# FNet mixing followed by an ELU layer in float32: the second layer's products as pairs of 64-column array tiles

## The chip, the cores and the metric

The kernel runs on one core of a Trainium2 chip. The metric is the device time of one execution in microseconds (us); lower is better. A span in a profile runs from the first to the last instruction of one profiled execution.

## What is computed

Everything is float32. For 8 sequences of 3008 rows with 256 channels, the reference takes the real part of a two-dimensional Fourier transform and feeds the resulting 24064 rows of 256 numbers to a two-layer network with 2048 hidden columns and an ELU between the layers:

```python
X = np.fft.fft(x, axis=1)
X = np.fft.fft(X, axis=2).real        # (8, 3008, 256) -> rows of 256
h = rows @ w_in                       # w_in 256 x 2048
g = np.where(h > 0.0, h, np.exp(np.minimum(h, 0.0)) - 1.0)
out = g @ w_out                       # w_out 2048 x 256
```

## The kernel before

**Symmetry.** The real transform is symmetric: row k and row 3008 - k come from the same two parts, a sum and a difference. So the kernel works on 8 x 1504 = 12032 columns, each standing for a pair of rows, and produces both rows of the pair. The channel transform is folded into the first layer's weights (`Wc`, `Ws`), and the sequence transform is done by matmuls with constant cosine and sine matrices (`MC`), whose results lie in two ring buffers `Rr` and `Ir`.

**Steps.** The columns are cut into 47 tiles of 256 (`TW`). For each tile there are 8 steps, 376 in all; a step handles two blocks of 128 hidden columns. In a step, TensorE does this:

- `mm_P` (L646): two products `H<-Rr,Wc`, each 128 weight columns by 256 moving columns, into a PSUM bank `H`.
- `mm_X1` (L739): three products of the second layer, for the step two periods earlier, into the banks pA and pB.
- `mm_Q` (L649): two products `H<-Ir,Ws`, added to the same bank `H`.
- `mm_X2` (L747): the other four products of the second layer, into pC and pD.

So a step has 4 products of the first layer and 7 of the second. The 7 stand for 8 block products: two hidden blocks times two output halves for each of the pair's two rows, combined in Strassen's way. The combined activations are seven blocks of 256 columns in the tile `G` (`blk(S, j)`, made by VectorE's ELU at L672 and by GpSimd's sums at L703 to L718, which all pass through the helper line L311), and the combined weights are `WT` (L358) beside the plain `w2`. A product of the second layer adds to one half, 256 columns, of a PSUM bank of 512 columns. The four banks pA to pD gather eight steps; then VectorE and ScalarE combine and transpose them (L757 to L800), and SyncE stores the rows.

All second-layer products go through one function, `prod` (L719). Its arguments are the accumulator bank `a`, the bank's half, the weights `lhsT` (128 x 128) and the number `j` of the block of G. All matmuls go through the helper `mm` (L300), so the profile shows them under L302 and they must be told apart by their tiles.

In float32 each matmul of the program runs as two weight loads (PEld LDWEIGHTS) and two matmul instructions (PE MATMUL): the profile's `x1504` for `H<-Rr,Wc` is 376 steps x 2 products x 2.

**Order.** The order on every engine is the program's order, written out by hand: each piece of a step has a due time (a list at L945 to L963, period 4.8), the pieces are sorted by it, and every instruction is pinned in that order. On TensorE the steady order is P, X1, Q, X2, P, and so on, with the sequence transform of a later sequence (`H<-MC,...`, some 28 of the steps carry a piece) between an X2 and the next P.

**Column tiles that are there already.** Four pieces use fewer than 128 weight columns and put their results in different 32-partition strips of one bank, so that they address different column tiles of the array: `dft_ext` (L561, 8 weight columns), `mid_mm` (L846), `mid_out` (L863) and `mid_pick` (L879), with 32 weight columns each. Each runs once. A fifth kind, `set_rest` (L461) and `whole_bank` (L895), multiplies one row of zeros.

Of the kernel before, what the change touches and what calls it, by code (L numbers as in the profile page):

```python
# [23 lines left out]
TW = 256  # L24
# [62 lines left out]
def kernel(  # L87
# [76 lines left out]
    w1 = {}  # L164

    class Chunk:
        """512 columns of weights: given as float64 words, they are rounded to the nearest
        float32 on chip; given as float32, they are loaded as they are."""

        def __init__(self, src, dst, raw, tmp):  # L170
            self.src, self.dst, self.raw_tags, self.tmp_tag = src, dst, raw, tmp
# [12 lines left out]
            )  # L184

        def parts(self):
            """low and high words, and the target, in columns of one shape"""
            dst = self.dst()
            raw = self.raw.rearrange("p (a b) w -> p a b w", a=dst.shape[1])
            return raw[:, :, :, 0], raw[:, :, :, 1], dst  # L190

        def fields(self):
            """The power of two 2^e as float32 bits (0 below float32's range); the low word
            as a fraction; the top 20 bits of the mantissa at float32's place."""
            if not wide:
                return
            lo, hi, dst = self.parts()
            t = spool.tile([128, 512], I32, tag=self.tmp_tag, bufs=1, name="pow2")
            self.t = t.rearrange("p (a b) -> p a b", a=dst.shape[1])
            pin(  # L200
                nc.vector.tensor_scalar(  # L201
                    out=self.t, in0=hi, scalar1=20, scalar2=0x7FF,
                    op0=ALU.logical_shift_right, op1=ALU.bitwise_and,
                )
            )
            act(self.t, self.t, func=AF.Relu, scale=2.0**23, bias=ebias)
            act(lo.bitcast(FP), lo.bitcast(U32), scale=2.0**-52)
            pin(
                nc.vector.tensor_scalar(
                    out=dst.bitcast(I32), in0=hi, scalar1=3, scalar2=0x7FFFF8,  # L210
                    op0=ALU.logical_shift_left, op1=ALU.bitwise_and,
                )
            )

        def join(self):
            """2^e * (1 + top bits) is exact; adding 2^e * the rest rounds."""
            if not wide:
                return
            lo, hi, dst = self.parts()
            vtt(dst.bitcast(I32), dst.bitcast(I32), self.t, ALU.bitwise_or)  # L220
            gtt(lo.bitcast(FP), lo.bitcast(FP), self.t.bitcast(FP), ALU.mult)
            gtt(lo.bitcast(FP), lo.bitcast(FP), dst, ALU.add)
# [77 lines left out]
    def mm(out_, lhsT, rhs, start, stop=True):  # L300
        pin(
            nc.tensor.matmul(  # L302
                out_, lhsT=lhsT, rhs=rhs, start=start, stop=stop, skip_group_check=True
            )
        )

    def vtt(o, a, b, op):
        pin(nc.vector.tensor_tensor(out=o, in0=a, in1=b, op=op))  # L308

    def gtt(o, a, b, op):  # L310
        pin(nc.gpsimd.tensor_tensor(out=o, in0=a, in1=b, op=op))  # L311

    def act(o, i, func=AF.Copy, **kw):
        pin(nc.scalar.activation(out=o, in_=i, func=func, **kw))  # L314


    def fold_weights():
        """w_in behind the channel DFT's cosine and sine halves."""
        n = len(w1_chunks)
        for c in range(n + 2):  # L320
            if c < n:
                if c >= 4:
                    w1_chunks[c].load()
                w1_chunks[c].fields()
            if 1 <= c <= n:
                w1_chunks[c - 1].join()
            if c >= 2:
                w1_chunks[c - 2].sign()
            if c >= 3 and c % 2:
                fold_block((c - 3) // 2)  # L330
        spread_last_row()

    def fold_block(q):
        cols = slice(q * 512, (q + 1) * 512)
        for part, dst in ((128, Ws), (0, Wc)):
            ps = bank("H")
            for h in range(2):
                mm(
                    ps,
                    CC[:, h * 256 + part : h * 256 + part + 128],  # L340
                    w1[q][:, h],
                    h == 0,
                    h == 1,
                )
            act(dst[:, cols], ps)

    def spread_last_row():
        nc.gpsimd.dma_start(out=wx_dr, in_=Ws[127:128, :])
        with nc.allow_non_contiguous_dma(reason="one row to columns"):
            nc.gpsimd.dma_start(  # L350
                out=wex, in_=wx_dr.rearrange("o (f p) -> p (o f)", p=128)
            )
# [307 lines left out]
        vtt(two(S.G[:, 0:512])[:, :, ::-1], two(S.E), two(S.H), ALU.subtract)  # L660

    def below(o, h):
        """max(-h, 0), so that exp(-o) = exp(min(h, 0)) cannot overflow."""
        act(o, h, func=AF.Relu, scale=-1.0)

    def exp_neg(ap):
        act(ap, ap, func=AF.Exp, scale=-1.0)

    def elu(o, h, e):
        """max(exp(min(h, 0)) - 1, h): exp(h) - 1 >= h, and 0 < h for positive h."""  # L670
        pin(
            nc.vector.scalar_tensor_tensor(  # L672
                out=o, in0=e, scalar=-1.0, in1=h, op0=ALU.add, op1=ALU.max
            )
        )

    def below_plus(i):
        S = steps[i]
        below(S.G[:, 512:1024], S.H)

    def below_minus(i):
        S = steps[i]
        S.M = bank("M")
        below(S.M, S.G[:, 0:512])
# [7 lines left out]
    def g_plus(i):  # L692
        S = steps[i]
        elu(S.G[:, 512:1024], S.H, S.G[:, 512:1024])

    def g_minus(i):
        S = steps[i]
        elu(S.G[:, 0:512], S.G[:, 0:512], S.M)

    def blk(S, j, n=1):  # L700
        return S.G[:, j * TW : (j + n) * TW]
# [16 lines left out]

    def prod(i, a, half, lhsT, j):  # L719
        S, T = steps[i], tiles[i // 8]  # L720
        mm(
            T.acc[a][:, half * TW : (half + 1) * TW],
            lhsT,
            blk(S, j),
            i % 8 == 0 and half == 0,
            i % 8 == 7,
        )

    def w2b(i, r, c):
        f = 2 * (i % 8) + r  # L730
# [8 lines left out]
    def mm_X1(i):  # L739
        if i % 8 == 0:  # L740
            T = tiles[i // 8] = Tile()
            T.acc = [bank(t) for t in ACC[0:2]]
        prod(i, 0, 0, w2b(i, 0, 0), 0)
        prod(i, 1, 0, w2b(i, 1, 0), 1)
        prod(i, 1, 1, wt(i, 1), 2)
# [107 lines left out]
    def mid_below():  # L853
        t = spool.tile([128, HALF + 1], FP, tag="rx", bufs=1, name="mid")
        state["mh"], state["mr"] = t[:, 0:512], t[:, 512:1024]
        below(state["mr"], state["mid"])

    def mid_g():
        h, r = state["mh"], state["mr"]
        elu(h, state["mid"], r)  # L860
        pin(nc.vector.transpose(out=r, in_=h))
# [38 lines left out]
    for _ in range(8):  # L900
        mm(bank("M"), zero[:, 0:128], zero[:, 0:1].to_broadcast([1, 512]), True)
    exp_neg(warm)
    fold_weights()
    EO, ops = fold_x(L_first, nc.vector, 1)

# [35 lines left out]
    T = PERIOD  # L941
# [192 lines left out]
```

## Time and profile before

| | |
|---|---|
| median of 2 runs | 2079.44 us (2078.43 and 2080.45) |
| span of the profiled execution | 2078.8 us |
| PE busy (matmuls, ends modelled) | 1983.5 us, 95% of the span, 8842 instructions |
| PEld busy (weight loads) | 1663.2 us, 80%, 8842 instructions |
| ScalarE, GpSimd, VectorE busy | 1393.9, 1385.7 and 976.6 us |
| mean granted TensorE clock | 0.983 |
| starts of step to step, steps 40 to 375, most of them | 4.753 us |

The span of the profiled execution is 0.6 us below the median of the runs; no other time is recorded for that execution, so sums below are made against 2078.8 us. PE means matmuls and PEld weight loads; these overlap. [...]the durations of successive matmuls overlap too: the distance between their starts tells their cost, and the duration doesn't. In a line such as `H<-w,mid 128*32 128x256 f32 x32`, 128*32 means 128 rows and 32 columns of weights, 128x256 the moving operand, and x32 the number of instructions.

### The profile page before, as it was taken

The page shows a single profiled execution, that of the slowest core. Times are in us where ns is not written, and L with a number is a line of the kernel's source. Part 1 is how long each engine was busy: PE and PEld are TensorE (multiplying, and loading weights), DVE is VectorE, ACT ScalarE, POOL GpSimd, SP SyncE. Part 2 cuts the span into 40 slices and gives each one's busy share as a digit, 9 for nine tenths or more (in the row PEclk, how much of TensorE's full clock was granted, in tenths as well). Part 3 has the DMA queues.
Part 4 walks back from the last instruction along what each step waited for, and adds up shares of the span by engine and source line. Part 5 has one row for each costly group of instructions (what it writes and reads, how often), then busy time and mean ns, then how long its engine had stood idle before and what let it go on. Part 6 is the DMA issues. An engine that isn't in the chain of part 4 may idle for free.

```text
span 2078.8 us, 27261 instructions
## 1 busy us (share of the span) xinstructions
PE 1983.5 (95%) x8842; PEld 1663.2 (80%) x8842; DVE 976.6 (47%) x1589; ACT 1393.9 (67%) x2761; POOL 1385.7 (67%) x1874
## 2 busy tenths in 40 slices
PE   3568999999999999999999999999999999999997
PEld 1247888888888888888888888888888888888886
DVE  2654454445444544454445445444544454445444
ACT  2255676777667766677667776677766776667775
POOL 3378775778657775678657786577756776555664
PEclk8799999999999999999999999999999999999999
DMA  8710211112100111012001120011110010100101
GB/s 217 117 51 11 57 49 16 16 33 62 23 11 18 46 44 23 11 22 77 11 19 20 35 57 18 15 17 54 42 24 11 18 18 17 16 11 11 21 11 21
DMA packets 253848, 71.07 MB, mean 34 GB/s; under 512 B 242370, under 2 KB 243162, under 8 KB 253194
## 3 DMA queue, kind: packets, MB, share of 16 engines
q1 hardware_dynamic: 251290, 56.73, 14.2%
q0 software_dynamic: 2416, 12.61, 1.9%
q8 instruction: 70, 1.15, 0.2%
q14 instruction: 72, 0.59, 0.1%
HBM read 44.45 MB, written 24.80 MB: 33 GB/s over the span
## 4 chain that ended last, share of the span: by engine, by line
PE 90%; DMA 2%; POOL 2%; DVE 2%; SPq 1%; ACT 1%; issue 1%; DVEq 0%; POOLq 0%; ACTq 0%
PE H L302 37%; PE pB L302 15%; PE pC L302 15%; PE pD L302 15%; PE pA L302 8%; DMA raw<-in_moe_w_out_dram 1%; POOL raw L311 1%; SPq L526 1%; DMA raw<-in_moe_w_in_dram 1%; POOL G L311 1%; DVE e L380 0%; DVE pow L201 0%; DVE w L229 0%; ACT G L314 0%; POOL WT L311 0%
## 5 line engine op out<-in xcount | busy, mean ns | idle before, releaser
L311 POOL TENSOR_TENSOR G<-G 128x256 f32<-128x256 f32 x1504 | 1080.5, 729 | 608.0 <-DVE G L672 473.6
L672 DVE SCALAR_TENSOR_TENSOR G<-G,H 128x512 f32<-128x512 f32 x376 | 258.5, 688 | 917.8 <-ACT G L314 917.7
L314 ACT ACTIVATE E<-H 128x512 f32<-128x512 f32 x376 | 224.5, 597 | 333.7 <-PE H L302 333.7
L302 PE MATMUL H<-Rr,Wc 128*128 128x256 f32 x1504 | 394.2, 385 | 8.8 <-ACT H L314 8.6
L302 PE MATMUL H<-Ir,Ws 127*128 127x256 f32 x1504 | 390.6, 382 | 1.4 <-ACT E L314 1.4
L302 PE MATMUL pC<-G,WT 128*128 128x256 f32 x1504 | 389.1, 381 | 0.0
L314 ACT ACTIVATE G<-H 128x512 f32<-128x512 f32 x376 | 224.6, 597 | 236.5 <-DVE G L308 236.5
L314 ACT ACTIVATE H<-Rb,wex 128x256 f32<-128x256 f32 x752 | 354.9, 472 | 16.9 <-DMA Rb<-r 3.1
L302 PEld LDWEIGHTS H<-Rr,Wc 128*128 128x128 f32 x1504 | 280.5, 190 | 54.1 <-ACT H L314 11.4
L302 PEld LDWEIGHTS H<-Ir,Ws 127*128 127x128 f32 x1504 | 287.6, 191 | 43.2 <-ACT E L314 2.5
L302 PEld LDWEIGHTS pC<-G,WT 128*128 128x128 f32 x1504 | 287.2, 191 | 40.7
L672 DVE SCALAR_TENSOR_TENSOR G<-M,G 128x512 f32<-128x512 f32 x376 | 256.9, 683 | 0.0
L308 DVE TENSOR_TENSOR G<-E,H 128x512 f32<-128x512 f32 x376 | 254.6, 677 | 4.6 <-PE H L302 4.0
L302 PE MATMUL pB<-G,WT 128*128 128x256 f32 x752 | 225.8, 382 | 16.7 <-POOL G L311 16.6
L314 ACT ACTIVATE G<-G 128x512 f32<-128x512 f32 x376 | 234.5, 624 | 0.0
L302 PE MATMUL pA<-G,w 128*128 128x256 f32 x752 | 224.4, 380 | 4.5 <-DVE G L672 2.4
L302 PE MATMUL pD<-G,WT 128*128 128x256 f32 x752 | 224.6, 380 | 0.0
L302 PE MATMUL pB<-G,w 128*128 128x256 f32 x752 | 224.1, 380 | 0.0
L302 PE MATMUL pD<-G,w 128*128 128x256 f32 x752 | 224.0, 380 | 0.0
L314 ACT ACTIVATE M<-G 128x512 f32<-128x512 f32 x376 | 224.0, 596 | 0.0
L314 ACT ACTIVATE M<-M 128x512 f32<-128x512 f32 x376 | 222.2, 591 | 0.0
L302 PEld LDWEIGHTS pB<-G,WT 128*128 128x128 f32 x752 | 142.8, 191 | 38.8 <-POOL G L311 19.7
(116 smaller groups left out, 1523.6 us busy)
## 6 DMA issues: line engine op xcount, KB each, us to landing
out_dram<-ot SPq DMA_DIRECT2D x504, 32.0 KB
xl<-in_x_dram SPq DMA_DIRECT2D x16, 768.0 KB
MC<-dft_mats SPq DMA_DIRECT2D x4, 1131.0 KB
raw<-in_moe_w_in_dram SPq DMA_DIRECT2D x8, 512.0 KB
raw<-in_moe_w_out_dram SPq DMA_DIRECT2D x8, 512.0 KB
out_dram<-ot SPq DMA_DIRECT2D x256, 2.0 KB
Rb<-r SPq DMA_DIRECT2D x10, 376.0 KB
out_dram<-ot SPq DMA_DIRECT2D x64, 28.0 KB
```

The source lines that it names most:

```text
L302: nc.tensor.matmul(out_, lhsT=lhsT, rhs=rhs, start=start, stop=stop, skip_group_check=True)
L308: pin(nc.vector.tensor_tensor(out=o, in0=a, in1=b, op=op))
L311: pin(nc.gpsimd.tensor_tensor(out=o, in0=a, in1=b, op=op))
L314: pin(nc.scalar.activation(out=o, in_=i, func=func, **kw))
L526: nc.sync.dma_start(out=t[:, s0:s1], in_=bass.AP(tensor=xt, offset=x.offset + row * ND + 128, ap=[[SEQ * ND, NB], [step * ND, s1 - s0], [1 ...
L672: nc.vector.scalar_tensor_tensor(out=o, in0=e, scalar=-1.0, in1=h, op0=ALU.add, op1=ALU.max)
```

## The change

Each second-layer product, 128 weight columns by 256 moving columns, is cut into four matmuls of 64 weight columns by 128 moving columns. The inner loop over `r` puts the two halves of the weight columns into partitions 0 to 63 and 64 to 127 of the accumulator, so into two different column tiles of the array; the outer loop over `c` cuts the moving columns. The mark that starts an accumulation goes to the first moving half alone. The weights, the blocks of G, the accumulators, the due times and everything outside `prod` stay as they are. Some docstrings are taken out as well, which makes no instruction and is left out here.

```diff
     def prod(i, a, half, lhsT, j):
         S, T = steps[i], tiles[i // 8]
-        mm(
-            T.acc[a][:, half * TW : (half + 1) * TW],
-            lhsT,
-            blk(S, j),
-            i % 8 == 0 and half == 0,
-            i % 8 == 7,
-        )
+        for c in range(2):
+            for r in range(2):
+                o = half * TW + c * 128
+                mm(
+                    T.acc[a][64 * r : 64 * r + 64, o : o + 128],
+                    lhsT[:, 64 * r : 64 * r + 64],
+                    S.G[:, j * TW + c * 128 : j * TW + c * 128 + 128],
+                    i % 8 == 0 and half == 0 and c == 0,
+                    i % 8 == 7,
+                )
```

In the changed program the matmuls of TensorE stand in the same order, with four in the place of each one of the second layer. The wait that stood before a product (for VectorE, or for GpSimd) stands before the first of its four. The order on the other engines is unchanged.

## Prediction

> **What bounds the kernel now.** I read the share of busy time, then the windows, then the list of waits, then the timeline of one step. The windows say where TensorE is the bound (columns: window, us, busy us of PE with its count, PEld, DVE, ACT, POOL, granted clock, DMA share, GB/s):
>
> ```profile
> 200.00:600.00 400.00, 398.13 (x1785) 337.02 (x1784) 185.59 (x305) 278.63 (x555) 280.97 (x379) 1.00 0.15 33
> 600.00:1000.00 400.00, 400.00 (x1819) 343.41 (x1818) 189.19 (x308) 287.15 (x571) 288.44 (x393) 1.00 0.15 33
> 1000.00:1400.00 400.00, 400.00 (x1798) 338.26 (x1797) 189.31 (x313) 278.37 (x555) 270.68 (x371) 1.00 0.12 25
> ```
>
> PE never stops at full clock; ScalarE and GpSimd work 70% of the time and VectorE 47%. The list of waits gives the whole kernel only 16.6 us of PE waiting for GpSimd before a second-layer product, and that falls before 210 us. So from about 180 us to the end, time added on TensorE is added to the kernel, and the other engines' work has room. The timeline of matmuls shows a step (start us, us from first start to last end):
>
> ```profile
> 1201.19 1.03 PE L302 MATMUL H<-Rr,Wc 128*128 128x256 f32 x4
> 1202.05 0.59 PE L302 MATMUL pA<-G,w 128*128 128x256 f32 x2
> 1202.48 0.59 PE L302 MATMUL pB<-G,w 128*128 128x256 f32 x2
> 1202.92 0.59 PE L302 MATMUL pB<-G,WT 128*128 128x256 f32 x2
> 1203.35 1.03 PE L302 MATMUL H<-Ir,Ws 127*128 127x256 f32 x4
> 1204.21 1.03 PE L302 MATMUL pC<-G,WT 128*128 128x256 f32 x4
> 1205.08 0.59 PE L302 MATMUL pD<-G,WT 128*128 128x256 f32 x2
> 1205.51 0.59 PE L302 MATMUL pD<-G,w 128*128 128x256 f32 x2
> 1205.94 0.38 PE L302 MATMUL H<-Rr,Wc 128*128 128x256 f32 x1
> ```
>
> From 1201.19 to 1205.94 is 4.75 us for 22 matmul instructions: 216 ns from start to start (0.86 us for four, 0.43 for two).
>
> The second thing to read is what a column tile costs here. The kernel has one run of 32-column tiles, the timeline of matmuls around `mid_out`, and the weight loads of the same stretch:
>
> ```profile
> 1889.76 0.59 PE L302 MATMUL pD<-G,w 128*128 128x256 f32 x2
> 1890.28 1.93 PE L302 MATMUL H<-w,mid 128*32 128x256 f32 x32
> 1892.15 0.70 PE L302 MATMUL H<-Rr,Wc 128*128 128x256 f32 x2
> ```
> ```profile
> 1890.28 1.45 PEld L302 LDWEIGHTS H<-w,mid 128*32 128x32 f32 x32 [0.33 <-PE pD L302]
> 1892.15 0.51 PEld L302 LDWEIGHTS H<-Rr,Wc 128*128 128x128 f32 x3 [0.41 <-issue]
> ```
>
> 32 matmuls of 256 columns start within 1.93 - 0.38 = 1.55 us. One after another they would take 32 x 0.216 = 6.9 us: four tiles run together, 8 rounds of 0.216. But the crossings cost. The last full matmul starts at 1889.76 + 0.22 = 1889.97, the first tiled one 0.31 us later in place of 0.216; on the way back the last tiled one starts at 1891.84, and the full one again 0.31 us later. A narrower window shows four tiled matmuls started by 1890.30, with 0.40 us each in place of 0.38: 24 ns of exposed weight load. The two full ones after the crossing take 0.70 in place of 0.59 us: 104 ns exposed. The rows by form give the loads' durations:
>
> ```profile
> L302 PEld LDWEIGHTS H<-Rr,Wc 128*128 128x128 f32 x1504 | 280.5, 190 | 54.1 <-ACT H L314 11.4 <-issue 2.3 <-ACT M L314 0.4
> ...
> L302 PEld LDWEIGHTS H<-w,mid 128*32 128x32 f32 x32 | 0.9, 109 | 0.8 <-PE pD L302 0.3
> ```
>
> [...](190 - 109) / 96 = 0.84 ns per column, on top of some 82 ns that don't delay the next load.[...]
>
> **The change part by part.**
>
> 1. *Tiled products.* 376 x 7 = 2632 products have 2 matmul instructions each, 5264; they become 8 each, 21056. They run in pairs, so a product is 4 rounds of 128 columns.[...] 4 x 109.4 = 437.5 against 432, so +5.4 ns per product, 38 ns per step.[...] From above, the loads: two loads of 64 columns per round take 54 ns each by the slope. Side by side or one after the other (107) they fit the round; only if a load's whole duration, 82 + 54 = 136 ns, had to pass before its matmul would a round be 138. I take 109.4, since the loads of `mid_out` overlap each other and each exposes only its columns' part.
> 2. *Crossings.* Each step goes full, tiled (X1), full (Q), tiled (X2): 2 ways in and 2 out, where before there were none. In: 310 - 216 = 93 ns[...], and an exposed load of 64 columns, 24 + (104 - 24) x 32 / 96 = 51: 144 ns. Out: 93, an exposed load of 128 columns, 104, and about 7 ns by which the second tile starts behind the first: 204 ns. 2 x (144 + 204) = 696 ns per step. This isn't hidden by anything: TensorE is the bound, and the loads that were prefetched under the matmul before lose that cover. Before the piece of a transform the crossing out merely moves.
> 3. *Waits and other engines.* No wait is added: those for VectorE and GpSimd stand before the first of four, and all end with more room, since the step becomes 0.73 us longer while ScalarE's and GpSimd's work stays at about 3.5 us. PSUM banks come free later by the same shift as everything else. 31,584 more instructions must be fetched; at the page's 1.74 MB for 27261, 64 bytes each, that is 2.0 MB in 2.3 ms, 0.9 GB/s beside a mean of 34. I cost it at nothing; it is the second rival if it isn't.
> 4. *Where it isn't paid.* The first seven steps, from 115 to 177 us, take 6 to 11 us each since w_out still arrives and GpSimd prepares it. Part of their 0.73 us may vanish there: I count 372 steps.
>
> Sum: (38 + 696) ns x 372 = 273 us. On the profiled 2078.8 us that is 2352 us; its distance to the median, 0.6 us, doesn't matter at this size.
>
> **Rivals.**
>
> - *Loads pace the rounds* (138 ns): 28 rounds x 28.6 ns = 0.80 us more per step, 298 us, so 2650. For it: no row here shows a load followed by its matmul within 136 ns. Against: [...]a full load is issued 108 ns behind the one before, while that one's record still runs (0.51 us for three loads).
> - *Supply of instructions.* A step goes from 44 loads and matmuls to 128, 43 ns each in a 5.49 us step and 27 in a tiled stretch. `mid_out` shows 64 within 1.55 us, 24 ns each, but once[...].[...] It decides above 43 ns. No run here shows the sustained rate.
> - *The pairs don't overlap.* 8 x 109.4 = 875 ns per product, 3.1 us more per step plus crossings: about 3490. Against it stands the four-fold overlap of `mid_out`; that was with 32-column tiles.
> - *The other side: the crossings are free.* [...]only 38 ns per step stay: 372 x 0.038 = 14 us, 2094, no measurable change. It needs a crossing below (2% of 2079 = 41.6 us, / 372 - 38 ns) / 4 = 18 ns. Against it: all crossings of 8- and 32-column tiles and of the one-row matmuls show about 92 ns.
>
> **How the numbers follow.** My forecast 0.70, with a range of its own of 2310 to 2420: 1 ns per round is 28 x 372 = 10.4 us, 10 ns per crossing is 15 us. Loads pace 0.10, supply 0.11, no overlap 0.03, free crossings 0.06. The range takes in forecast and pacing, 0.80: 2310 to 2660. 2% is about what a measurement can tell here. Faster[...]: 0.01. Same: 0.05. Slower: 0.94.
>
> **What would show it.** The profile after should have 21056 tiled matmuls in starts of two, 109 ns from pair to pair; PEld gaps of about 0.2 us (0.31 minus a round) at X1 and X2 and 0.2 to 0.3 after them; steps of 5.49 us; PE still without waits for other engines. Rounds near 138 would say that the loads pace, uneven ones near or above 170 that the supply does, single starts every 109 that there is no overlap, and steps under 4.85 that crossings are free.

## The result and the profile after

The changed kernel takes 2345.85 us, the median of two runs (2344.35 and 2347.34), against 2079.44 before: a ratio of 1.126, with an interval of 1.122 to 1.131. The profiled span is 2345.6 us. The forecast was 2352.

The windows of the changed kernel (columns as before: window, us, then busy us of PE, PEld, DVE, ACT and POOL with their counts, granted clock, DMA share, GB/s):

```profile
600.00:1000.00 400.00, 400.00 (x4409) 310.11 (x4410) 171.66 (x274) 245.03 (x487) 237.61 (x327) 1.00 0.11 22
1000.00:1400.00 400.00, 400.00 (x4497) 313.03 (x4493) 168.64 (x267) 250.98 (x497) 253.06 (x342) 1.00 0.14 32
```

PE is still the bound at full clock, and the others have more room: ScalarE falls from 283 to 248 us in 400 (mean of these two windows against those of before). PE's busy share doesn't show what happened, since a matmul's modelled duration covers the gaps (a matmul of the step of before lasts 380 ns there, and the next one starts after 216). The timeline of matmuls does. One step of the changed kernel:

```profile
1200.54 1.13 PE L302 MATMUL H<-Rr,Wc 128*128 128x256 f32 x4
1201.60 0.66 PE L302 MATMUL pA<-G,w 128*64 128x128 f32 x8
1202.09 0.61 PE L302 MATMUL pB<-G,w 128*64 128x128 f32 x8
1202.52 0.61 PE L302 MATMUL pB<-G,WT 128*64 128x128 f32 x8
1203.06 1.13 PE L302 MATMUL H<-Ir,Ws 127*128 127x256 f32 x4
1204.12 1.09 PE L302 MATMUL pC<-G,WT 128*64 128x128 f32 x16
1205.05 0.61 PE L302 MATMUL pD<-G,WT 128*64 128x128 f32 x8
1205.48 0.61 PE L302 MATMUL pD<-G,w 128*64 128x128 f32 x8
1206.02 1.13 PE L302 MATMUL H<-Rr,Wc 128*128 128x256 f32 x4
```

From one P to the next is 5.48 us, against 4.75 before. A product inside a stretch, pB's first to pB's second, takes 0.43 us, just what it took whole. The time is at the four places where 128*128 and 128*64 meet. The four full matmuls take 1.06 us to the next line in place of 0.86, the last product of a stretch 0.54 in place of 0.43, and the first one gets longer by 0.05 (pA 0.49 in place of 0.43, pC 0.93 in place of 0.87). Twice 0.20, 0.11 and 0.05 make the 0.73 us by which the step is longer. The weight loads of the same step show the same four gaps:

```profile
1201.60 0.42 PEld L302 LDWEIGHTS pA<-G,w 128*64 128x64 f32 x8 [0.33 <-issue]
...
1203.06 0.73 PEld L302 LDWEIGHTS H<-Ir,Ws 127*128 127x128 f32 x4 [0.17 <-ACT G L314]
1204.12 0.85 PEld L302 LDWEIGHTS pC<-G,WT 128*64 128x64 f32 x16 [0.33 <-issue]
...
1206.02 0.30 PEld L302 LDWEIGHTS H<-Rr,Wc 128*128 128x128 f32 x2 [0.17 <-issue]
```

Before each stretch no load runs for 0.33 us, after it for 0.17. The prediction named about 0.2 and 0.2 to 0.3 as signs; the gaps are at the places that it named, but their sizes were wrong. Where `ACT G` is named, that instruction is only the last event before the load; the other gap of the same kind, at 1206.02, names none.

### The profile page after: what moved, and what is told of

Same layout as the page of the kernel before. It is cut to its first block, busy times and chain, and to the rows that moved or that the text cites. A ratio compares the mean times of both kernels' runs of the same rounds, so it can differ in the third digit from the quotient of the medians.

```text
span 2345.6 us, 58892 instructions
## 1 busy us (share of the span) xinstructions
PE 2252.6 (96%) x24634; PEld 1739.2 (74%) x24634; DVE 1004.3 (43%) x1589; ACT 1399.0 (60%) x2761; POOL 1385.9 (59%) x1874
## 4 chain that ended last, share of the span: by engine, by line
PE 92%; DMA 2%; SPq 2%; POOL 1%; DVE 0%; ACT 0%; issue 0%; DVEq 0%; ACTq 0%; POOLq 0%
PE H L302 39%; PE pC L302 16%; PE pB L302 14%; PE pD L302 14%; PE pA L302 9%; SPq L526 1%; DMA raw<-in_moe_w_out_dram 1%; DMA MC<-dft_mats 1%; POOL raw L311 1%; SPq L547 1%; DMA x<-in_x_dram 1%; DMA xe_dr<-x 0%; POOL G L311 0%; POOL WT L311 0%; ACT raw L314 0%
## 5 line engine op out<-in xcount | busy, mean ns | idle before, releaser
L302 PE MATMUL H<-Rr,Wc 128*128 128x256 f32 x1504 | 426.0, 406 | 10.4 <-ACT H L314 10.3
L302 PE MATMUL H<-Ir,Ws 127*128 127x256 f32 x1504 | 427.6, 407 | 1.4 <-ACT E L314 1.4
L302 PEld LDWEIGHTS pC<-G,WT 128*64 128x64 f32 x6016 | 323.6, 137 | 124.8 <-issue 124.8
L302 PE MATMUL pC<-G,WT 128*64 128x128 f32 x6016 | 414.9, 280 | 0.0
L302 PEld LDWEIGHTS pA<-G,w 128*64 128x64 f32 x3008 | 156.6, 136 | 127.8 <-issue 123.8
L302 PE MATMUL pA<-G,w 128*64 128x128 f32 x3008 | 247.1, 285 | 3.5 <-DVE Ir L308 2.1
L302 PE MATMUL pB<-G,WT 128*64 128x128 f32 x3008 | 228.9, 273 | 14.6 <-POOL G L311 14.6
L302 PE MATMUL pD<-G,WT 128*64 128x128 f32 x3008 | 229.8, 274 | 0.0
L302 PE MATMUL pD<-G,w 128*64 128x128 f32 x3008 | 229.0, 273 | 0.0
L302 PE MATMUL pB<-G,w 128*64 128x128 f32 x3008 | 228.1, 273 | 0.0
```

Source lines behind the costliest of these rows:

```text
L302: nc.tensor.matmul(out_, lhsT=lhsT, rhs=rhs, start=start, stop=stop, skip_group_check=True)
```

## The experiments

Nine runs, in three groups on three chips. The kernel before took 2081.8, 2084.1 and 2086.7 us beside them, so an absolute expectation made against 2079.4 is 2 to 7 us low from that alone. The better measure is the length of a plain step, one without a piece of the sequence transform (median from one first X1 matmul to the next), which repeats within a few ns: 4.753 us before and 5.480 after. The theory: crossings between full matmuls and tiled ones cost 696 ns per step and the products themselves almost nothing. A round is the time from one matmul's start to the next one's on the same tile.

**X1 next to X2, in the changed kernel and in the kernel before.** The copy that reads pA moves with it, as it has to follow the last X1.

```diff
-            (2 * T + 0.87, mm_X1),
+            (2 * T + 3.03, mm_X1),
...
-            (1.45, comb_copy),
+            (3.10, comb_copy),
```

> The changed kernel with X1 moved next to X2, so that a step goes into the 64-column tiles once and comes back once instead of twice. If the crossings carry the cost (348 ns for a way in and out), a step falls from 5.480 to 5.132 us and the time is 2346 - 0.348 x 368 = 2218 us. If the number or the shortness of the instructions carries it, nothing changes (2346), and if the supply of instructions has been saved by the pauses between the two stretches, the seven products in one stretch of 112 loads and matmuls become slower, above 2346.

> Control: the kernel before with the same move of X1 and no tiles. Every theory expects the time before, 2079 us, steps of 4.753 us.

Measured: 2564.2 us with tiles (1.233, 1.228 to 1.237), and 2427.0 for the control without any (1.165, 1.161 to 1.170). Both expectations missed, since the move itself costs 345 us. The list of waits of the control, us in total, times and longest, has an entry that hardly existed before:

```profile
PEld H L302 <- ACT E L314: 422.8, 376, 4.7
PE H L302 <- ACT E L314: 271.5, 376, 4.3
```

In every step `mm_Q` has to wait until ScalarE has copied P's result (`dbl`, E<-H, 0.6 us) out of the bank that Q adds to. X1 stands between them as cover: with it the copy ends in time, without it P and Q lie 1.066 us apart instead of 0.216, and Q's load is exposed. We had not seen that edge of the order; it would have been in the list of steps as 'X1 covers P, copy, Q'.

The pair is still a clean test, as both have this wait. A step takes 5.705 us without tiles and 6.085 with, so tiles with one crossing pair per step cost 0.380 us, where the theory says 0.348 for the crossings and 0.031 for 28 rounds. With two pairs they cost 0.727. Halving the crossings halves the cost.

**Short rounds without tiles.** The loop over `r` goes, the one over `c` stays:

```diff
-                    T.acc[a][64 * r : 64 * r + 64, o : o + 128],
-                    lhsT[:, 64 * r : 64 * r + 64],
+                    T.acc[a][:, o : o + 128],
+                    lhsT,
```

> Each product cut into two matmuls of 128 moving columns with the full 128 weight columns: the short rounds without column tiles, so without crossings. If the crossings carry the cost, only the constant part of the rounds is left: 4 rounds of 109 ns per product, 31 ns per step, 2091 us; a load of 128 columns takes 107 ns by the slope and just fits the round. If the short rounds or the doubled instructions carry the cost, it stays near 2346. If a load's whole duration of 190 ns paces the rounds, 28 x 81 ns = 2.27 us per step, about 2920 us.

Measured: 2127.9 us, 1.020 (1.015 to 1.025); a step of 4.855 us. Most of the 266 us is gone, so short rounds and 60% more loads and matmuls aren't the cause. But it isn't free, and 2091 was missed: 0.102 us per step, where 0.031 was expected, is 7 x 4 rounds of 111.7 ns, not 109. The timeline of matmuls shows it in a product that takes 0.445 instead of 0.43 us (two products later by 0.89):

```profile
1200.08 0.61 PE L302 MATMUL pA<-G,w 128*128 128x128 f32 x4
1200.53 0.61 PE L302 MATMUL pB<-G,w 128*128 128x128 f32 x4
1200.97 0.61 PE L302 MATMUL pB<-G,WT 128*128 128x128 f32 x4
```

The changed kernel's rounds have the same 128 moving columns over loads of 64 and take 109 ns, so the wider load is the likely cause. Right after a crossing a load of 128 columns follows the one before it after 108 ns (traces before and after); the round is some 4 ns longer. The last experiment but one has rounds as near to their loads at another size.

**Tiles with 256 moving columns.** The loop over `c` goes, the one over `r` stays; the moving operand is `blk(S, j)` again.

```diff
-        for c in range(2):
-            for r in range(2):
+        for r in range(2):
```

> Pairs of 64-column tiles with the whole 256 moving columns: half the instructions of the changed kernel, the same crossings. If the crossings carry the cost, 2346 - 0.031 x 368 = 2334 us, steps of 5.449 us. If the number of instructions carries it, about half of the 266 us goes, near 2210.

Measured: 2331.8 us, 1.120 (1.116 to 1.124); a step of 5.444 us against 5.449 expected. With half the instructions of the tiled products a step is 36 ns shorter, not far from 7 x (436 - 432), the 28 ns by which four rounds of 128 moving columns are longer than two of 256, and the crossings' cost stays.

**Everything in a step tiled.** On top of the change, the first layer is cut into pairs too:

```diff
-            mm(
-                S.H[:, j * TW : (j + 1) * TW],
-                W[0:M, f * 128 : (f + 1) * 128],
-                ring[0:M, cols(i)],
-                False,
-            )
+            for r in range(2):
+                mm(
+                    S.H[64 * r : 64 * r + 64, j * TW : (j + 1) * TW],
+                    W[0:M, f * 128 + 64 * r : f * 128 + 64 * r + 64],
+                    ring[0:M, cols(i)],
+                    False,
+                )
```

> The changed kernel with the first layer in pairs of 64-column tiles too, 256 moving columns each, so that a step never leaves the tiling. If the crossings carry the cost, a plain step is 4.753 + 0.031 = 4.784 us and, with one way out before each of the 28 transform pieces, the time is about 2095 us, although all matmuls of the steps are tiled. If working in column tiles itself costs, it stays at or above 2346.

Measured: 2111.7 us, 1.013 (1.010 to 1.017); a plain step of 4.787 us against 4.784 expected. The timeline of a step has no gap left:

```profile
1200.80 0.61 PE L302 MATMUL pB<-G,w 128*64 128x128 f32 x8
1201.24 0.61 PE L302 MATMUL pB<-G,WT 128*64 128x128 f32 x8
1201.68 1.03 PE L302 MATMUL H<-Ir,Ws 127*64 127x256 f32 x8
1202.54 1.05 PE L302 MATMUL pC<-G,WT 128*64 128x128 f32 x16
```

More tiling made 234 us of the 266 vanish. So it isn't tiles that cost but changing between them and the full array. Three things account for most of the distance from 2095 to 2111.7. There are 56 transform pieces, not 28 (7 sequences x 4 transforms x 2 halves: the section on the kernel before and the expectation have the number wrong), and each costs 0.15 us more than before as a crossing has been added: 8.4 us instead of 4. The runs of that chip were some 5 us slower. And the profiled run, one of four, lost 6.1 us in step 258: a product waited 4.2 us for GpSimd, behind a DMA of the last sequence's rows, and then the granted clock was 0.50 from 1494.3 to 1497.5 us. The profiled runs of the two kernels below with smaller tiles and shorter rounds lost 3.1 and 6.1 us in the same step, those of the kernels before and after nothing.

**Loops exchanged.** `for r` outside, `for c` inside.

> The changed kernel with the two loops of a product exchanged, so that both moving halves of the first tile come before those of the second. If TensorE looks past at least eight loads and matmuls for work for the idle tile, the pairs still overlap and the time stays at about 2346 us. If matmuls start strictly in program order, a product takes 6 rounds instead of 4: 7 x 2 x 109 ns = 1.53 us per step more, about 2910 us.

Measured: 2384.4 us, 1.144 (1.141 to 1.148); a step of 5.580 us. In this run TensorE started work for the idle tile ahead of earlier instructions: in a stretch's first product the second tile's first matmul starts 13 ns after the first tile's first, while three matmuls and three loads that stand before it have not started. Strict order would have taken 7.0 us per step. It costs 100 ns per step all the same: after the first product the second tile comes to run half a round behind (starts 52 and 57 ns apart instead of 7 and 102), so that each of the two stretches ends some 50 ns later.

**Smaller tiles.** `range(4)` and 32 for the two halves of the weights:

```diff
-            for r in range(2):
+            for r in range(4):
...
-                    lhsT[:, 64 * r : 64 * r + 64],
+                    lhsT[:, 32 * r : 32 * r + 32],
```

> Four 32-column tiles instead of two of 64, still 128 moving columns: 240 loads and matmuls per step instead of 128, 16 in a round of 109 ns. If the crossings carry the cost and the supply is ample, a way in exposes 24 instead of 51 ns and a way out starts 13 ns later: 2346 - 2 x 0.014 x 368 = 2336 us. If instructions come no faster than the 27 ns that the changed kernel has shown, the tiled stretches double: 3.05 us per step more, about 3480 us.

Measured: 2341.9 us, 1.124 (1.121 to 1.127); a step of 5.453 us, just the 27 ns less that the narrower exposed loads and later last tile make. The timeline has 16 matmuls of a product (and 16 loads) in 0.44 us:

```profile
1202.67 0.62 PE L302 MATMUL pD<-G,WT 128*32 128x128 f32 x16
1203.11 0.62 PE L302 MATMUL pD<-G,w 128*32 128x128 f32 x16
```

That is 14 ns per load or matmul, twice the rate of the changed kernel, and no slower. So the supply doesn't pace the changed kernel; where its limit lies, no run shows.

**Shorter rounds.** `range(4)` over the moving columns, 64 each:

```diff
-        for c in range(2):
+        for c in range(4):
...
-                o = half * TW + c * 128
+                o = half * TW + c * 64
```

> Two 64-column tiles with 64 moving columns[...]. If the two tiles' loads run side by side (54 ns each by the slope), a product is 446 instead of 436 ns, 70 ns per step, 2372 us. If the loads of the two tiles follow one another (107 ns per round), 56 rounds x 51 ns = 2.9 us per step more, about 3410 us.

Measured: 2426.4 us, 1.165 (1.161 to 1.169); a step of 5.685 us. With 696 ns for the crossings, the rest of 0.932 us, 0.236, is 7 x (8 x 58.2 - 432) ns: rounds of 58.2 ns, where the 446 ns per product expected are rounds of 55.8 (an estimate from the traces of before and after: matmuls of 512 and 256 moving columns start 429 and 216 ns apart, 0.832 ns per column, and 109 less 64 such columns is 55.8). So the two tiles' loads did run side by side (one after the other, at the loads' 0.84 ns per column: 107). Right after a crossing a tile's second load follows its first after 55 ns (64 columns) or 108 (128), so the rounds of 58.2 and 111.7 are both 3 to 4 ns longer than that, which fits loads that pace the round again. It isn't shown: more time for such short matmuls themselves would look the same, and narrower loads under the same 64 moving columns were not run. Nor is it shown where the 3 to 4 ns come from. The changed kernel's rounds of 109 ns are well above 58.2.

**Crossings taken out of the kernel before.** Its own one-row matmuls of zeros are crossings too, if the 93 ns more before them (410 after the last transform matmul, 317 from one of those to the next) have the same cause. Here they have 128 rows:

```diff
-    zero = cpool.tile([1, 264], BF, tag="zero")
+    zero = cpool.tile([128, 264], BF, tag="zero")
...
-zero[:, 0:1].to_broadcast([1, 512])
+zero[:, 0:1].to_broadcast([128, 512])
```

> The kernel before, with the matmuls of zeros at the end of each transform piece on 128 rows of zeros instead of one. The one-row matmul stands 410 ns after the transform's last matmul instead of 317, and the next full one starts 158 ns later with 104 ns of exposed load. If these are crossings too[...], they go: (410 - 317) + (158 + 104 - 59) = 296 ns for each of 28 pieces, 8.3 us, about 2071 us, faster than the kernel before. If the drain is due to the change from float32 to bfloat16, or to the waits there, nothing changes: 2079.

Measured: 2067.9 us against 2086.7 beside it, 0.991 (0.989 to 0.992). It is faster than both kernels, by more than expected, because there are 56 pieces. A piece becomes 247 ns shorter, not 296: the zeros stand 316 instead of 410 ns after the transform's last matmul (94 saved), and from the zeros' start to the first unexposed weights of P it takes 58 + 51 instead of 158 + 104 (153 saved; 51 stay exposed, as the load's 108 ns are longer than the 58 between the two starts). The timelines show the gaps, first of the kernel before:

```profile
279.08 1.11 PE L302 MATMUL H<-MC,e 128*128 128x377 f32 x3
280.13 0.23 PE L302 MATMUL H<-zero 1*128 1x135 bf16 x1
280.29 1.13 PE L302 MATMUL H<-Rr,Wc 128*128 128x256 f32 x4
281.25 0.59 PE L302 MATMUL pA<-G,w 128*128 128x256 f32 x2
```

and of this run:

```profile
285.82 2.06 PE L302 MATMUL H<-MC,e 128*128 128x377 f32 x6
287.72 0.22 PE L302 MATMUL H<-zero 128*128 128x135 bf16 x1
287.78 1.08 PE L302 MATMUL H<-Rr,Wc 128*128 128x256 f32 x4
288.70 0.59 PE L302 MATMUL pA<-G,w 128*128 128x256 f32 x2
```

The zeros are bfloat16 in both, so the change of type isn't the cause of the delay. 56 x 0.247 is 13.8 us, and in the profiled runs the steps from 15 on, which hold all the pieces, are 14.4 us shorter. Before them, steps 11 to 14 came 2.4 us shorter, of which 1.7 are step 14: in the kernel before its granted clock was 0.50 from 215.7 to 218.9 us, after a wait of 1.9 us, and here it was 1.00. What is left of the measured 19 (16 to 23 by the interval) was not found; the time before the first step differs from run to run by as much.

## Why the prediction was right

1. *Tiled products.* The term was 5.4 ns per product and the measured one is about 4: four rounds of 109.0 make 436. The term's round of 109.4 ns was the author's estimate, and the trace of before bears it out: matmuls of 512 moving columns (`H<-w,CC`) start 429 ns apart at full clock and those of 256 216, so 256 columns take 213, and 216 less half of that is 109.5. That 64-column tiles pair as the 32-column ones of `mid_out` did was read from another size, and held: the two starts of a pair are 7 ns apart. Three runs (256 moving columns, 32-column tiles, everything tiled) each give the expected step within 5 ns from the same terms, which include the crossings.
2. *Crossings.* The term was 144 ns in and 204 out. In the changed kernel the first tiled pair starts 309 ns after the last full matmul, and the second pair 160 ns after the first: 93 of delay and 51 of exposed load. On the way out, 202 ns from the last tile's start to the full matmul, and 320 to the next: 93, 7 late and 104 exposed. Together these are 348 ns for a way in and out, as forecast. What TensorE does in the 93 ns, which an expectation above calls a drain, the traces don't show; they show the later start. The control pair, the all-tiled kernel and the kernel without one-row matmuls show it as a cause: one pair of crossings gives half the cost, none gives none, and taking those of before away makes the kernel before faster.
3. *Waits and other engines.* Nothing was added: TensorE waited no longer for GpSimd than before (14.6 us against 16.6, the last number of the lines below, before and after), and none of it after 400 us. But that list of waits was made for the change, not for the step's order: the copy between P and Q, covered by X1, was overlooked, and both expectations of the experiment built on it failed.

```profile
L302 PE MATMUL pB<-G,WT 128*128 128x256 f32 x752 | 225.8, 382 | 16.7 <-POOL G L311 16.6
...
L302 PE MATMUL pB<-G,WT 128*64 128x128 f32 x3008 | 228.9, 273 | 14.6 <-POOL G L311 14.6
```

4. *Where it isn't paid.* The seven early steps took 2.2 us of their 5.1. Steps 13 and 14 gave 2.3 us back (1.37 and 0.96 shorter), where 0.73 longer each was forecast: in the kernel before, step 13 waits for a DMA into `Rb`, and step 14 is the one that ran at a granted clock of 0.50. In the changed kernel step 13 is only 0.06 us longer than a plain one, and the clock stays at 1.00. So the bound on TensorE, which the prediction took from about 180 us, holds from step 15 at 222 us. From there 259.4 us were added, 0.72 per step: 0.727 in a plain one, 0.5 to 0.6 in seven around the middle rows, some of whose crossings were paid before.

The total is closer than its terms. Between the profiled spans 266.8 us were added, 6.2 less than the 273 of the forecast. The steps up to 15 and the end brought 5.6 us less than counted, and the steps from 15 on 4.8 less, half of it 0.007 us in each plain step. But the first step began 4.2 us later, and that was luck: in the nine runs it began between 5 us earlier and 10 us later than before.

Of the rivals, the supply fell with the 32-column tiles (14 ns per load or matmul, where it decides above 43), the pacing by whole loads (138 ns) with rounds of 58 and 109, the pairs that don't overlap with the starts 7 ns apart and the product of 0.43 us, and the free crossings with the gaps.

## What to carry to other kernels

Where TensorE is the bound, count the places where the matmul stream changes between the full array and column tiles, and price each as measured: here 93 ns of delay plus the first load that lost its cover, 51 ns at 64 columns and 104 at 128. Tiles brought nothing in this kernel, since a product took 436 ns in pairs and 432 whole, so the crossings were pure cost. If tiles are needed, tile the neighbours too, or put the tiled stretches together, but look first at what the stage between them was covering. A one-row matmul in a stream of full ones cost a crossing here as well, and padding it to all rows was cheaper by 247 ns per piece.

## What the runs showed of the hardware

- Into and out of tiles of 8, 32 or 64 columns, the first matmul started 93 to 94 ns later than without a crossing (309 ns in place of 216, 409 in place of 316), and 93 to 96 ns later into one row (312 in place of 216).
- A crossing exposed the first load after it: 24, 51 or 104 ns for 32, 64 or 128 columns.
- Loads of different column tiles ran side by side: 32 of 109 ns each, 32 columns wide, within 1.45 us. In steady rounds a tile's loads of 64 columns came 58.2 ns apart (under 64 moving columns) and the full array's of 128 columns 111.7 (under 128), 0.84 ns per column; right after a crossing the second one came after 55 and 108 ns.
- With the loops exchanged, matmuls of an idle tile started ahead of earlier ones in the program that waited for their own tile, past three matmuls and three loads, 13 ns after the first tile's first.
- A stretch of 32-column tiles took 14 ns per load or matmul, and a product in it 0.44 us, as in the changed kernel.
